# Where the sums of layer one's weight blocks are made: sixteen copies and sixteen adding transfers moved into layer zero's mixing

## The chip, the cores and the metric

One core of one Trainium2 chip. The metric is the device time of one execution in microseconds. TensorE is called PE here, VectorE DVE, ScalarE ACT, GpSimd POOL and SyncE SP, as in the profile.

## The reference

Two kinds of layers take turns, twice each: a linear attention (A) and a gated mixer (B). The change sits in B. "Layer zero" and "layer one" below are the first and the second pair.

```python
def _B_ref(x, w_in, w_sp, b_sp, w_out):          # x: 2048 x 512
    z = _gelu(jnp.einsum("bsd,df->bsf", x, w_in))
    z1 = z[..., :Fh]                              # 2048 x 896
    z2 = _layernorm(z[..., Fh:], axis=-1)         # 2048 x 896
    g = jnp.einsum("ts,bsf->btf", w_sp, z2) + b_sp[None, :, None]   # w_sp: 2048 x 2048
    return jnp.einsum("bsf,fd->bsd", z1 * g, w_out)

x = x + _A_ref(_layernorm(x, axis=-1), A_wqkv, A_wo)
x = x + _B_ref(_layernorm(x, axis=-1), B_w_in, B_w_sp, B_b_sp, B_w_out)
x = x + _A_ref(_layernorm(x, axis=-1), A_wqkv, A_wo)
x = x + _B_ref(_layernorm(x, axis=-1), B_w_in, B_w_sp, B_b_sp, B_w_out)
```

All is in float32. Each product runs as three passes on PE over values split in two: a high part that ACT copies into PE's format and a low part that DVE makes by subtraction (`split`, `mm3`, `acc`).

## The kernel before, in words

The order of the instructions on each engine is the order in which the program names them; nothing reorders them. An engine that waits holds up all that stands behind it on that engine, and so does SP, from whose queue nearly all transfers are issued. Tiles come from numbered slots that are given out in turn: 22 pages (`pg`, 256 KB), 6 quads (`qd`), 4 large ones (`bg`) and 8 banks of PSUM.

A pair of layers has four stages: `P1` (queries, keys and their sums), a transition, `P2` (the rest of attention, then z1 and z2), and `P4` (the mixing with `w_sp`, then the product with `w_out`). Before the first `P1` stands a start of its own.

The mixing is done with seven products in place of eight, called P1 to P7 in `P4.ORDER` (P2, P1, P6, P7, P4, P5, P3), over half matrices. Some of the products need sums of blocks of `w_sp`. These sums are made once: in layer zero, `Sums.tick` loads blocks, adds them on POOL and stores them (`s` tiles). In layer zero each product has 8 steps, 56 in all. In layer one the products P2 and P4 are divided once more (`DIVIDED`): each becomes seven smaller ones with 14 steps. These need sums of quarter blocks: for P2 and for P4 there are four sums (m = 1 to 4), each in two parts (q). `Sums.halve` makes them in DRAM, without an engine that computes: SP's queue copies a block of `w_sp` to a tile `hP2...` or `hP4...`, and POOL's queue then sends an adding transfer that adds another block, or another sum, to it (m = 2 takes the sum of m = 1, m = 4 that of m = 2). That makes 16 copies and 16 adds of 512 KB each. In the profile they appear as `hP<-in_wsp_dram` and `hP<-hP`.

Where `halve` is called before: eight copies (P2's) after output products 0 to 7 of layer zero and eight adds (P2's) after products 8 to 15, in `join`; P4's copies in steps 3 to 10 of layer one's `P1`; P4's adds in steps 4 to 11 of layer one's `P2`.

A step g of the mixing (`P4.run`) does this, in this order: `fetch(g + 4)` asks SP for the weight block four steps ahead; `sp(g + 2)` splits the block that is needed two steps ahead (`wsp`: ACT at L889, DVE at L890) and the rows of z2 for it (`zsp`); `mm(g)` runs 24 matmuls (18 in P6, P7 and P3) at L1055 to L1057; in steps 0 to 18 a `Sums.tick`; and `tick` multiplies one finished unit of g with z1 on POOL (`gate`, L1093) and asks for the next z1 page. A quad is free for the next load when `wsp` has split it. In the eight steps of P3 `wpiece` also loads one piece of `w_out` and splits it at once.

After the steps come 16 output products `o(i)` with `zsplit` two ahead of them (L109 on ACT, L112 on DVE), an addition to x at L1163 and a store at L1165. In layer zero `join(i, nxt)` follows each: it loads x tiles, query and key weights (`wk` at i = 8, `wq` at i = 10, four pieces each) and splits them for layer one's `P1`.

In layer one `P4.run` first asks for steps 0 to 2, then runs what is left of z1 (`p2.f()`, seven products at this point) beside the first splits of z, then asks for step 3, for the four bias rows (`loadb`, L1086, each one spread over 128 partitions) and for the steps from 4 on.

Of the kernel before, what the change touches and what calls it, by code (L numbers as in the profile page):

```python
# [12 lines left out]
AF = mybir.ActivationFunctionType  # L13
OP = mybir.AluOpType
# [38 lines left out]
DIVIDED = ((), ("P2", "P4"))  # L53
# [3 lines left out]
def mixer_kernel(ctx: ExitStack, tc: tile.TileContext, x_in, wqkv, wo_d, win1_d, win2_d, wsp_d, bsp_d, wout_d,  # L57
# [45 lines left out]
    def behind(ins, other):  # L103

        tc.add_manual_dep(ins.ins, other.ins.name, mybir.DependencyInfo(
            mybir.DependencyClass.Sync, mybir.DependencyReason.DATA))
# [149 lines left out]
    class P1:  # L256
# [180 lines left out]
        def run(self, sums):  # L437
            side = deque([self.win2] * NF)
            ND = NT - DEFER
            for s in range(1, NT + 2):  # L440
                self.loadx(s + 3)
                self.turn.load(s + 1)
                if 2 <= s < NT:
                    self.T_high(s)
                if s == 1:
                    if not self.kb:
                        self.K(0)
                    self.K(1)
                elif 2 < s <= NT:
                    self.K(s - 1)  # L450
                self.ln_a(s + 2)
                if 2 <= s < NT:
                    self.T_low(s)
                if s <= NT:
                    self.K_phi(s - 1)
                if s <= ND:
                    self.Q(s - 1)
                if s == NT + 1:
                    self.late()
                if s <= NT:  # L460
                    self.xsplit(s - 1)
                    self.K_split(s - 1)
                self.ln_b(s + 2)
                if s <= ND:
                    self.Q_phi(s - 1)
                if s >= 2:
                    self.Gmm(s - 2)
                if s == NT + 1:
                    self.late_phi()
                if s == 6:  # L470
                    self.wv, self.wo = (quads.get([P, 4, 512]) for _ in range(2))
                    nc.sync.dma_start(self.wv, wqkv[:, 1024:1536].rearrange("(c p) f -> p c f", p=P))
                    nc.sync.dma_start(self.wo, wo_d.rearrange("(c p) f -> p c f", p=P))
                if self.L == 1 and 3 <= s < 11:
                    sums.halve(13 + s)
                if s > 3 and side:
                    side.popleft().piece()
                if s > 2 and side:
                    side[0].fetch()
# [64 lines left out]
    class P2:  # L544
# [152 lines left out]
        def run(self, sums):  # L697
            w1 = self.win1
            for s in range(1, NT + 3):
                self.loadx(s + 1)  # L700
                self.qturn.load(s + 1)
                if s in self.qturn.by_pe:
                    self.c(s - 1)
                    self.b_high(s)
                    self.c2(s - 1)
                    self.p1.late_phi_b()
                    self.b_low(s)
                    if s >= 2:
                        self.d_high(s - 2)
                        self.d_low(s - 2)  # L710
                    self.p1.late()
                    self.c3(s - 1)
                    self.a2(s + 2)
                    self.p1.late_phi_a()
                    self.a(s + 3)
                else:
                    if s < NT:
                        self.b_high(s)
                    self.a2_den(s + 2)
                    if s < NT:  # L720
                        self.b_low(s)
                    if s <= NT:
                        self.c(s - 1)
                        self.c2(s - 1)
                    if s == NT:
                        quads.put(*self.W2)
                        pages.put(self.zbc)
                    self.a2_mul(s + 2)
                    late = s - 2 in self.xturn.by_pe
                    if late:  # L730
                        self.d_high(s - 2)
                        self.d_low(s - 2)
                    if s <= NT:
                        self.c3(s - 1)
                    self.a(s + 3)
                    if s <= NT + 1 and not late:
                        self.d_high(s - 2)
                        self.d_low(s - 2)
                if s >= 4:
                    self.e4(s - 4)  # L740
                self.xturn.load(s - 1)
                if s >= 3:
                    self.e(s - 3)
                    self.e2(s - 3)
                    self.e3(s - 3)
                self.f()
                self.f()
                self.fq.extend(self.fnext)
                self.fnext = []
                w1.piece(True)  # L750
                w1.fetch()
                if self.L == 0 and s > 4:
                    sums.tick()
                if self.L == 1 and 3 < s < 12:
                    sums.halve(20 + s)
                if s >= NT + 1:
                    self.p4.fetch(s - NT - 1)
            self.e4(NT - 1)
            self.win2.free()


    class Sums:
# [3 lines left out]
        def __init__(self):  # L766
            self.s = {(m, k): dram.tile([P, 2, 512], F32, name=f"s{m}_{k}") for m in range(1, 5) for k in range(HT)}
            self.todo = deque((k, j, h) for k in range(HT) for j in range(2) for h in range(2))
            self.ahead = deque(self.todo)
            self.raw, self.made, self.done = {}, [], []  # L770
            self.slots = pages
            self.parts, self.halves = [], {}
            for p in DIVIDED[1]:
                for q in range(2):
                    for m in range(1, 5):
                        self.halves[p, m, q] = dram.tile([2, P, 512], F32, name=f"h{p}_{m}_{q}")
            self.parts = [(what, p, m, q) for p in DIVIDED[1] for what in ("copy", "add") for m in (1, 3, 2, 4)
                          for q in range(2)]

        def fetch(self):  # L780
# [2 lines left out]
                at = ((j, k), (j, k + HT), (2 + j, k)) if h == 0 else ((2 + j, k + HT),)  # L783
                self.raw.setdefault((k, j), []).extend(load(wsp_d[n, s], self.slots) for n, s in at)

        def halve(self, n):

            if n >= len(self.parts):
                return
            what, p, m, q = self.parts[n]  # L790
            row = 2 if p == "P2" else 0
            j, s = {1: ((1, 0), (1, 4)), 3: ((0, 0), (1, 0)), 2: ((0, 0), None), 4: ((0, 4), None)}[m][what == "add"] or (0, 0)
            src = wsp_d[row + j, HT + s + 2 * q:HT + s + 2 * q + 2]
            if what == "copy":
                nc.sync.dma_start(self.halves[p, m, q], src)
            else:
                if m in (2, 4):
                    src = self.halves[p, m // 2, q]
                nc.gpsimd.dma_start(self.halves[p, m, q], src, accum_op=OP.add, max_dma_last_dim=4096)

        def store(self):

# [30 lines left out]
    class P4:  # L833
# [50 lines left out]
        def wsp(self, g):  # L884
            if g >= len(self.steps):
                return
            r = self.raw.pop(g)
            w = quads.get([P, 2, 2, 512], F32R)
            nc.scalar.activation(w[:, 0], r, AF.Copy)  # L889
            nc.vector.tensor_sub(w[:, 1], r, w[:, 0].bitcast(F32))  # L890
            quads.put(r)
            self.w[g] = w
# [277 lines left out]
        def run(self, nxt):  # L1170
            p2 = self.p2
            self.fetch(2)
            self.sp(0)
            ahead = deque()
            if self.div:
                self.zpart(0)
# [12 lines left out]
            p2.win1.free()  # L1189
            self.sp(1)  # L1190
            self.fetch(3)
            if self.div:
                self.loadb()
            self.gb = [bigs.get([P, NF, 512]) for _ in range(NCHK)]
            n = len(self.steps)
            for g in range(n):
# [11 lines left out]
                    self.sp(g + 2)  # L1208
                if g < 19:
                    self.sums.tick()  # L1210
                if g == 3 and not self.div:
                    self.loadb()
                if p in self.div:
# [29 lines left out]

        def join(self, i, nxt):

            self.sums.halve(i)
            if i in (5, 6, 7, 10):
                nxt.loadx((5, 6, 7, 10).index(i))
            if i in (7, 8, 9):
                nxt.ln_a(i - 7)  # L1250
                nxt.ln_b(i - 7)
            if i in (8, 10):
                for _ in range(4):
                    (nxt.wk if i == 8 else nxt.wq).fetch()
            if i in (11, 12):
                nxt.turn.load(i - 11)
            if 10 <= i < 14:
                nxt.wk.piece()
            if 11 <= i < 15:
                nxt.wq.piece()  # L1260
            if i == 14:
                nxt.T(0)
            if i == 15:
                nxt.T(1)
# [46 lines left out]
```

## Time and profile before

| | |
|---|---|
| runs shown | 1403.86, 1406.55 and 5764.37 us, median 1406.55 |
| the profiled execution | 1403.85 us, span 1402.1 us, mean granted clock 0.995 |
| PE busy | 1380.4 us, 98% of the span |
| DVE, ACT, POOL busy | 889.9, 587.1, 398.8 us |
| transfers | 248.76 MB, 177 GB/s over the span |
| of these, on POOL's queue | 8.39 MB, 3.5% of the time of 16 DMA engines |

The span runs from the first to the last instruction. Layer zero's mixing ends and its output products begin at about 624 us, layer one's `P1` begins at 716 us, layer one's mixing at 1056 us. A row of the timeline shows start, duration, engine, line, operation, written tile `<-` read tiles, shapes, count, and in brackets the idle time of the engine just before it with what ended it. SPq and POOLq rows are issues of transfers; a row `DMA` in the chain is a transfer on its way.

### The profile page before, as it was taken

How to read it: one execution, taken by the hardware profiler on the slowest of the kernel's cores; microseconds unless marked ns; L12 is line 12 of the kernel's file. 1: busy time of each engine (PE TensorE's matmuls, PEld its weight loads, DVE VectorE, ACT ScalarE, POOL GpSimd, SP SyncE). 2: the span in 40 equal slices, each digit the busy share in tenths (PEclk: the TensorE clock that was granted, in tenths of full speed). 3: DMA queues.
4: the chain of work that ended last, by engine and by line, in shares of the span. 5: the costliest groups of instructions: out<-in, count | busy, mean ns of one | idle time of the engine just before them, and what ended most of it. 6: DMA issues, size and time to landing. Idle time of an engine off the chain costs nothing.

```text
span 1402.1 us, 17453 instructions
## 1 busy us (share of the span) xinstructions
PE 1380.4 (98%) x6182; PEld 1150.6 (82%) x6182; DVE 889.9 (63%) x1331; ACT 587.1 (42%) x893; POOL 398.8 (28%) x506
## 2 busy tenths in 40 slices
PE   9999999999999999999799999999999999999998
PEld 7888888888888888888578888888887888878887
DVE  6665868752688766563266658776436757886532
ACT  6664533343323333340156645443345323633420
POOL 3233455444367102131213233543110020021300
PEclk9999999999999999999899999999999999999999
DMA  5641267866988433347947522787336444454432
GB/s 163 194 120 54 97 225 249 270 217 212 331 306 301 173 120 113 129 180 255 246 151 237 198 68 81 188 241 198 131 115 203 151 161 162 148 176 150 172 120 90
DMA packets 148344, 248.76 MB, mean 177 GB/s; under 512 B 12448, under 2 KB 51104, under 8 KB 148000
## 3 DMA queue, kind: packets, MB, share of 16 engines
q1 hardware_dynamic: 145952, 239.26, 51.3%
q0 software_dynamic: 2304, 8.39, 3.5%
q8 instruction: 48, 0.79, 0.2%
q14 instruction: 40, 0.33, 0.1%
HBM read 179.70 MB, written 84.67 MB: 189 GB/s over the span
## 4 chain that ended last, share of the span: by engine, by line
PE 88%; DVE 4%; DMA 3%; ACT 2%; issue 1%; POOL 1%; SPq 1%; ACTq 0%; DVEq 0%; POOLq 0%
PE bank L125 17%; PE bank L123 17%; PE bank L124 17%; PE bank L1056 12%; PE bank L1057 12%; PE bank L1055 12%; DMA pg<-in_wqkv_dram 2%; DVE qd L890 1%; DVE st L186 1%; PE bank L517 1%; DMA qd<-hP 1%; PE bank L528 0%; DMA pg<-in_x_dram 0%; SPq L100 0%; ACT qd L889 0%
## 5 line engine op out<-in xcount | busy, mean ns | idle before, releaser
L1056 PE MATMUL bank<-qd,pg 128*128 128x512 f32 x784 | 305.6, 390 | 1.5 <-DVE qd L890 1.5
L1055 PE MATMUL bank<-qd,pg 128*128 128x512 f32 x784 | 305.3, 389 | 0.7 <-ACT qd L889 0.7
L1057 PE MATMUL bank<-qd,pg 128*128 128x512 f32 x784 | 305.2, 389 | 0.0
L890 DVE TENSOR_TENSOR qd<-qd,qd 128x1024 fp32r<-128x1024 f32 x124 | 168.9, 1363 | 137.1 <-ACT qd L889 137.0
L889 ACT ACTIVATE qd<-qd 128x1024 fp32r<-128x1024 f32 x124 | 131.1, 1057 | 191.9 <-PE bank L1057 151.7
L1093 POOL TENSOR_TENSOR bg<-bg,pg 128x512 f32<-128x512 f32 x56 | 83.5, 1511 | 409.0 <-DVE bg L1103 147.8
L1056 PEld LDWEIGHTS bank<-qd,pg 128*128 128x128 f32 x784 | 147.2, 188 | 33.9 <-DVE qd L890 3.4
L1055 PEld LDWEIGHTS bank<-qd,pg 128*128 128x128 f32 x784 | 147.2, 188 | 32.0 <-ACT qd L889 1.1
L1057 PEld LDWEIGHTS bank<-qd,pg 128*128 128x128 f32 x784 | 147.2, 188 | 30.8 <-DVE pg L929 0.4
L125 PE MATMUL bank<-qd,pg 128*128 128x512 f32 x384 | 149.7, 390 | 0.0
L199 ACT ACTIVATE pg<-pg,nb,rs 128x512 f32<-128x512 f32 x63 | 51.0, 810 | 172.4 <-POOL nb L193 172.3
L190 POOL TENSOR_SCALAR rs<-mv 128x1 f32<-128x1 f32 x96 | 27.2, 284 | 331.2 <-DVE mv L188 330.5
L123 PE MATMUL bank<-qd,pg 128*128 128x512 f32 x288 | 112.5, 391 | 0.3 <-DVE pg L112 0.2
L124 PE MATMUL bank<-qd,pg 128*128 128x512 f32 x288 | 112.3, 390 | 0.2 <-DVE qd L112 0.2
L809 POOL TENSOR_TENSOR pg<-pg,pg 128x512 f32<-128x512 f32 x64 | 93.3, 1458 | 55.9 <-DMA pg<-in_wsp_dram 48.0
L125 PE MATMUL bank<-wo,qd 128*128 128x512 f32 x224 | 89.0, 397 | 9.6 <-DVE qd L112 9.6
L123 PE MATMUL bank<-bg,qd 128*128 128x448 f32 x256 | 94.2, 368 | 0.4 <-ACT qd L109 0.4
L124 PE MATMUL bank<-bg,qd 128*128 128x448 f32 x256 | 93.6, 366 | 0.0
L125 PE MATMUL bank<-bg,qd 128*128 128x448 f32 x256 | 93.6, 365 | 0.1
L123 PE MATMUL bank<-wo,qd 128*128 128x512 f32 x224 | 88.5, 395 | 2.7 <-ACT qd L109 2.7
L124 PE MATMUL bank<-wo,qd 128*128 128x512 f32 x224 | 88.1, 393 | 0.0
L125 PE MATMUL bank<-qd,bg 128*128 128x512 f32 x224 | 87.5, 390 | 0.0
(137 smaller groups left out, 2555.3 us busy)
## 6 DMA issues: line engine op xcount, KB each, us to landing
qd<-s SPq DMA_DIRECT2D x64, 512.0 KB, 3.3
qd<-in_wsp_dram SPq DMA_DIRECT2D x44, 512.0 KB, 4.0
pg<-in_wsp_dram SPq DMA_DIRECT2D x64, 256.0 KB, 4.9
s<-pg SPq DMA_DIRECT2D x64, 256.0 KB, 4.5
pg<-x SPq DMA_DIRECT2D x64, 256.0 KB, 3.9
z<-pg SPq DMA_DIRECT2D x56, 256.0 KB, 3.0
pg<-z SPq DMA_DIRECT2D x56, 256.0 KB, 3.7
x<-pg SPq DMA_DIRECT2D x48, 256.0 KB, 3.3
```

Source lines behind the costliest of these rows:

```text
L123: nc.tensor.matmul(out, ah, bh, start=start, stop=False)
L124: nc.tensor.matmul(out, ah, bl, start=False, stop=False)
L125: nc.tensor.matmul(out, al, bh, start=False, stop=stop)
L190: nc.gpsimd.tensor_scalar(rs, mv[:, 1:2], LN_EPS, None, op0=OP.add)
L199: nc.scalar.activation(y, x, AF.Identity, bias=nb, scale=rs)
L809: nc.gpsimd.tensor_tensor(t, a, b, op=OP.add)
L889: nc.scalar.activation(w[:, 0], r, AF.Copy)
L890: nc.vector.tensor_sub(w[:, 1], r, w[:, 0].bitcast(F32))
L1055: m(out, h[:, o], w[:, 0, j, :], start=start, stop=False, skip_group_check=True)
L1056: m(out, h[:, o], w[:, 1, j, :], start=False, stop=False, skip_group_check=True)
L1057: m(out, l[:, o], w[:, 0, j, :], start=False, stop=stop, skip_group_check=True)
L1093: nc.gpsimd.tensor_tensor(u, u, z1, op=OP.mult)
```

## The change

The list of the parts is put in another order, all 16 copies first (P2's, then P4's), then all 16 adds. The three places that called `halve` drop it. It is called instead in layer zero's mixing, once in each of the steps 19 to 50, behind the matmuls of the step and ahead of its `tick`: copies in steps 19 to 34, adds in 35 to 50. Each add gets a dependency on the instruction `mark`, the ACT half of the latest weight split, so that POOL issues it only when ACT has come to that step. In layer one the bias rows are asked for right behind the first split, ahead of the rest of z1. PE, DVE and ACT run the same instructions in the same order as before; the copies move on SP's queue, the adds on POOL's, and from the bias rows on some pages have other numbers.

```diff
@@ P1.run
-                if self.L == 1 and 3 <= s < 11:
-                    sums.halve(13 + s)
@@ P2.run
-                if self.L == 1 and 3 < s < 12:
-                    sums.halve(20 + s)
@@ Sums.__init__
-            self.parts = [(what, p, m, q) for p in DIVIDED[1] for what in ("copy", "add") for m in (1, 3, 2, 4)
+            self.parts = [(what, p, m, q) for what in ("copy", "add") for p in DIVIDED[1] for m in (1, 3, 2, 4)
                           for q in range(2)]
@@ Sums.halve
-        def halve(self, n):
+        def halve(self, n, after):
-            if n >= len(self.parts):
+            if not 0 <= n < len(self.parts):
                 return
...
-                nc.gpsimd.dma_start(self.halves[p, m, q], src, accum_op=OP.add, max_dma_last_dim=4096)
+                behind(nc.gpsimd.dma_start(self.halves[p, m, q], src, accum_op=OP.add, max_dma_last_dim=4096), after)
@@ P4.wsp
-            nc.scalar.activation(w[:, 0], r, AF.Copy)
+            self.mark = nc.scalar.activation(w[:, 0], r, AF.Copy)
@@ P4.run
             self.fetch(2)
             self.sp(0)
+            if self.div:
+                self.loadb()
...
             self.sp(1)
             self.fetch(3)
-            if self.div:
-                self.loadb()
...
                 if g < 19:
                     self.sums.tick()
+                if nxt is not None:
+                    self.sums.halve(g - 19, self.mark)
@@ P4.join
-            self.sums.halve(i)
```

## The prediction

> **What bounds the kernel now.** I read the busy times first, then the stretches of 35 us, then the waits and the chain where a stretch was short of full.
>
> ```profile
> PE 1380.4 (98%) x6182; PEld 1150.6 (82%) x6182; DVE 889.9 (63%) x1331; ACT 587.1 (42%) x893; POOL 398.8 (28%) x506
> ```
>
> TensorE is busy for all but 21.7 us of the span of 1402.1, and the change leaves its instructions and their order as they were. So there is little to win: those 21.7 us, and what the clock loses after a stop. I then looked where they lie (columns: stretch, length, busy us and count of PE, PEld, DVE, ACT, POOL, granted clock, DMA share, GB/s).
>
> ```profile
> 525.00:560.00 35.00, 35.00 (x156) 29.01 (x155) 21.81 (x30) 10.94 (x13) 7.64 (x5) 1.00 0.35 119
> ...
> 595.00:630.00 35.00, 35.00 (x156) 28.99 (x155) 23.28 (x29) 16.61 (x23) 12.16 (x8) 1.00 0.48 173
> 630.00:665.00 35.00, 35.00 (x156) 29.01 (x155) 12.85 (x17) 2.87 (x3) 3.03 (x4) 1.00 0.78 263
> 665.00:700.00 35.00, 26.20 (x108) 21.23 (x108) 9.89 (x14) 7.08 (x9) 9.62 (x16) 0.85 1.00 239
> 700.00:735.00 35.00, 31.59 (x131) 25.41 (x130) 20.97 (x34) 17.97 (x29) 4.01 (x9) 0.95 0.47 154
> ...
> 910.00:945.00 35.00, 35.00 (x164) 30.34 (x163) 24.58 (x43) 16.06 (x27) 15.69 (x26) 1.00 0.87 236
> ```
>
> 665 to 735 holds 12.2 us of the idle time, at a lower clock, with DMA at 1.00. That is the output product of layer zero, where the first adding transfers run. In layer one's first stages (910 to 945), where the second half of them runs, TensorE is full: taking them out there wins nothing. The chain and the DVE's timeline tell what happened at 665:
>
> ```profile
> 673.05 13.88 DMA pg<-in_wqkv_dram
> 686.99 15.14 DMA pg<-in_wqkv_dram
> 702.24 0.64 ACT qd L109
> ```
>
> ```profile
> 671.37 0.69 DVE L1163 TENSOR_TENSOR pg<-pg,bank 128x512 f32<-128x512 f32 x1 [2.04 <-PE bank L125]
> 676.13 0.69 DVE L1163 TENSOR_TENSOR pg<-pg,bank 128x512 f32<-128x512 f32 x1 [1.81 <-PE bank L125]
> 693.13 0.69 DVE L1163 TENSOR_TENSOR pg<-pg,bank 128x512 f32<-128x512 f32 x1 [11.15 <-DMA pg<-x]
> ...
> 716.21 0.69 DVE L1163 TENSOR_TENSOR pg<-pg,bank 128x512 f32<-128x512 f32 x1 [1.47 <-PE bank L125]
> ```
>
> Line 1163 ends each of the 16 output products, one every 4.76 us until 676.13 (the eleventh; five follow). Then the loads of layer one's query and key weights take 14 and 15 us and a load of x is late too; ACT and DVE wait for them in front of the split (L109, L112) that feeds the next product. The last product should end at 676.13 + 5 x 4.76 = 699.93 and ends at 716.21: **16.3 us late**. The adding transfers stand beside it:
>
> ```profile
> 675.63 1.79 POOL L799 DMA_DIRECT2D hP<-in_wsp_dram  x2
> 676.79 1.46 POOL L799 DMA_DIRECT2D hP<-hP  x1
> 679.24 0.81 POOL L799 DMA_DIRECT2D hP<-hP  x1 [0.98 <-DMA hP<-in_wsp_dram]
> ```
>
> ```profile
> DMA to landing us min/median/max: 5.8/8.2/14.1
> ...
> q0 software_dynamic: 2304, 8.39, 3.5%
> ```
>
> Nothing paces them there: four are issued from 675.63 to 680.05, on top of the weight loads. The 16 of them hold all 16 DMA engines for 3.5% of 1402.1 us, so about 3.1 us each (an estimate, and from a crowded stage, so rather high).
>
> **The change, part by part.** *Taken out of the output stage:* 8 copies and 8 adds. Worth 16.3 us if nothing else is late. What is late next is seen from the product's own split on ACT and DVE:
>
> ```profile
> 676.44 0.94 ACT L109 ACTIVATE qd<-bg 128x896 fp32r<-128x896 f32 x1
> ...
> 677.48 1.09 DVE L112 TENSOR_TENSOR qd<-bg,qd 128x896 fp32r<-128x896 f32 x1 [0.66 <-ACT qd L109]
> ```
>
> ACT wants the first weight piece behind this split, at 677.4. Four weight loads are under way from 673.05; a 256 KB load without an add beside it lands in 3.2 us (row below), so they are there by about 678. DVE's work per product is 0.69 + 1.09 and two weight pieces of some 0.7, 3.2 us of 4.76. Bounds: 16.3 us won, or 16.3 - 5 where half of the late waits stay; I take **-16.3**, since the products before 676 ran at full pace with the same loads of x and stores.
>
> *Put into layer zero's mixing:* the copies at steps 19 to 34 (about 451 to 520), the adds at steps 35 to 50 (520 to 604), one a step. (The split at 536.78 below is the one made in step 38; steps of products 4 and 5, up to step 47, take 5.44 us as these two rows show, those of 6, 7 and 3 have 18 matmuls in place of 24 and take 4.08.) A copy goes to SP's queue behind that step's loads and waits for no engine; an add goes to POOL's queue and waits for ACT's split of that step (L889). Behind the add wait POOL's gates (L1093), and behind a gate the page that it frees; such pages are written again three steps later at the earliest, 12 us, so a gate held for one or two us is covered. The cover of the loads that feed the splits:
>
> ```profile
> 531.34 1.06 ACT L889 ACTIVATE qd<-qd 128x1024 fp32r<-128x1024 f32 x1 [1.78 <-PE bank L1057]
> 536.78 1.06 ACT L889 ACTIVATE qd<-qd 128x1024 fp32r<-128x1024 f32 x1 [1.79 <-PE bank L1057]
> ...
> L889 ACT ACTIVATE qd<-qd x37: 1043/1061/1066, 442.8 to 611.1; 128x1024 fp32r<-128x1024 f32 x37
> ...
>   PE bank L1057: 39.6, 24
> ...
> qd<-s SPq DMA_DIRECT2D x64, 512.0 KB, 3.3
> ...
> L890 DVE TENSOR_TENSOR qd<-qd,qd 128x1024 fp32r<-128x1024 f32 x124 | 168.9, 1363 | 137.1 <-ACT qd L889 137.0
> ```
>
> From 440 to 660 these splits wait for TensorE (24 times) and never for a transfer. A load is issued when the split three steps before it has freed its buffer, so it has three steps less the 2.4 us of that split (1.06 on ACT, 1.36 on DVE): 14 us at 5.44 a step, 10 us at 4.08. It needs 3.3. DMA in these stretches stands at 0.35, 1.9 us of a step of 5.44; with an add that is 5.0 of 5.44, 91%. A copy costs between 1.4 us ((0.78 - 0.48) x 35 / 7.4 copies, from the stretches at 630 and 595) and 3.7 us (all of the 0.78): below 14 and 10 either way. These parts cost 0.
>
> The price of an add's company shows in layer one, in two stretches of the DMA issues, without (876 to 884) and with one (904 to 914):
>
> ```profile
> pg<-x SPq DMA_DIRECT2D x1, 256.0 KB, 3.2
> ...
> pg<-x SPq DMA_DIRECT2D x1, 256.0 KB, 7.1
> ```
>
> About 4 us more for a load. That matters in one place, the last product's steps 48 to 50, where a piece of the output weight is loaded and split in the same step (`wpiece`), with ACT standing still until it lands:
>
> ```profile
> 596.27 0.38 SPq L100 DMA_DIRECT2D pg<-in_wout_dram  x1
> ...
> 600.30 0.63 ACT L109 ACTIVATE wo<-pg 128x512 fp32r<-128x512 f32 x1 [3.62 <-DMA pg<-in_wout_dram]
> 600.84 1.05 ACT L889 ACTIVATE qd<-qd 128x1024 fp32r<-128x1024 f32 x1
> ...
> 608.72 0.63 ACT L109 ACTIVATE wo<-pg 128x512 fp32r<-128x512 f32 x1 [3.84 <-DMA pg<-in_wout_dram]
> 609.26 1.05 ACT L889 ACTIVATE qd<-qd 128x1024 fp32r<-128x1024 f32 x1
> ```
>
> The split at 600.84 is for step 52, which starts at about 607.5 (536.8 + 10 x 5.44 + 4 x 4.08): some 4 us to spare after the 2.4 us that the split needs. A late split also frees its buffer late, SP's queue stops on it, and the piece behind it on SP is asked for late. Followed from step to step, 3 us more per piece costs 0 to 0.4 us of TensorE, 4 us costs 1 to 2.5, 6 us costs 5 to 6.5, 8 us costs 9 to 10.5 (the first where only pieces up to 606 are slowed, the second up to 612). I take **+1.5**, nearest to the row of 4 us; the bounds are 0 and +10.
>
> The Trainium skill, "DMA: Bandwidth & Descriptors", section on the anatomy of a SWDGE transfer, fits 2.0 us plus bytes over 436 GB/s; for 512 KB that is an estimate of 3.2 us. By it an add would be gone before the next step's load, this term would be 0 and the time 1386.5. The trace disagrees (5.8 to 14.1 us to landing), so I keep the row.
>
> *The bias rows of layer one asked for sooner.* Now four loads stand on SP's queue between two loads of the sums; the rows are SP's timeline, the chain, ACT's timeline and TensorE's waits from 1050 to 1090, and ahead of them one wait from 660 to 720 that is used further down:
>
> ```profile
> PE bank L123 <- ACT qd L109: 2.7, 1, 2.7
> ...
> 1057.94 1.92 SPq L1086 DMA_DIRECT2D pg<-in_bsp_dram  x4
> ...
> 1059.95 7.12 DMA qd<-hP
> ...
> 1067.09 1.06 ACT L889 ACTIVATE qd<-qd 128x1024 fp32r<-128x1024 f32 x1 [2.40 <-DMA qd<-hP]
> ...
> PE bank L1056 <- DVE qd L890: 0.8, 1, 0.8
> PE bank L1055 <- ACT qd L889: 0.7, 1, 0.7
> ```
>
> Moved ahead of seven remaining products of the first gate half, they go out at about 1045; the load of the sums goes out 2 us earlier and alone. It then has the 2.4 us that ACT waited, and the two waits of TensorE go: **-1.5**. The four pages are held longer, but those taken are free by then. Bounds 0 and -1.6.
>
> **Sum**, against the profiled execution's own 1403.85 us (span 1402.1 and 1.8 around it): -16.3 - 1.5 + 1.5 gives 1387.5. The runs shown are 1403.86, 1406.55 and one far outlier, so their median of 1406.55 stands 2.7 above the lower of the two; I put 0.5 on top: **1388**.
>
> **The rivals.** *The output weight's pieces come late.* For it: they are the one load with no cover. Against: only three adds meet them. At 6 to 8 us more, 5 to 10 us lost, and 1.4 us for the clock (16.3 less the 12.2 of idle time is 4 us over three stops): 1392 to 1399.
>
> The Trainium skill, "TensorE: Matmul & The Clock Gate", part on the clock gate, lets the clock fall only after some 3.4 us of idle; stops of 1 to 2 us would then cost themselves alone, and the 1.4 would drop out: 1390 to 1398. The trace leaves it open: after the wait of 2.7 us, itself close behind a longer one, 700 to 735 shows 0.95.
>
> *The weight loads at 672 stay slow without the adds.* For it: x loads and stores and eight weight pieces remain. Against: 0.78 with copies did not slow TensorE. It would leave some 5 us: 1393.
>
> *The adds fill the DMA engines in the mixing (slower).* At 3.1 us an add the step is 91% full. If beside the split loads an add takes 6 us, a step needs 7.9 us in place of 5.44 and TensorE waits for split loads: 2.5 us in 13 steps, 3.9 in three, 44 us, less 18: 1430. It decides from 3.5 us per add on (where a step is full), and eats the whole gain at about 4.7. For it: 8.2 us to landing. Against: 910 to 945 runs with adds at 0.87 and TensorE full.
>
> *The change brings only the bias rows' gain or nothing there:* 1386 to 1389.5, inside the forecast.
>
> **How the numbers follow.** Forecast 1384.5 to 1391: 0.70. Pieces late: 0.15 (1392 to 1399). Weight loads stay slow: 0.10. Adds fill the engines: 0.05. The range 1384 to 1398 takes in the forecast and most of the two next. A difference of 2%, 28 us, is about what a measurement of this kernel can tell from no change. More than 28 us faster would need more than all the idle time and slow clock: 0.01. More than 28 us slower is a part of the last case: 0.03. Within: 0.96.
>
> **What would show it right or wrong.** Right: no adds after 620; the weight loads land in under 6 us; line 1163 keeps 4.76 us to its sixteenth; 630 to 735 full. The splits L889 from 440 to 610 still wait for TensorE. The load of the sums at the start of layer one's mixing lands in about 4 us. Wrong: waits of L889 or L890 for `qd` transfers in steps 35 to 50, ACT's waits for the output weight above 6 us and a PE wait at 607 to 620, or a hole at the layers' border that names the weights again.

## The result, and the profile after

The changed kernel takes 1387.49 us (median of 1386.75, 1388.24, 1392.31 and 1386.45) against 1405.2 us for the kernel before, run on the same chip. The ratio is 0.9884 [0.9852, 0.9917] (it leaves out the one far outlier of the kernel before, 5764 us, which that median still counts): 1.2% faster, so within 2%, and 0.5 us from the forecast of 1388. The profiled execution is the one of 1386.75 us. Its page, busy times and POOL's queue:

```profile
span 1384.9 us, 17460 instructions
...
PE 1376.4 (99%) x6182; PEld 1149.0 (83%) x6182; DVE 893.1 (64%) x1331; ACT 587.6 (42%) x893; POOL 396.7 (29%) x506
...
q0 software_dynamic: 2304, 8.39, 3.4%
```

TensorE's idle time fell from 21.7 to 8.5 us, with the same 6182 matmuls. The stretches of 35 us show where (columns as before: stretch, length, PE, PEld, DVE, ACT, POOL, granted clock, DMA share, GB/s):

```profile
595.00:630.00 35.00, 34.21 (x150) 27.80 (x149) 24.53 (x28) 16.33 (x24) 17.35 (x13) 1.00 0.71 214
630.00:665.00 35.00, 35.00 (x156) 28.99 (x155) 14.54 (x17) 3.59 (x4) 2.60 (x2) 1.00 0.42 140
665.00:700.00 35.00, 35.00 (x156) 29.01 (x155) 19.64 (x29) 12.62 (x18) 3.17 (x9) 1.00 0.66 214
700.00:735.00 35.00, 35.00 (x156) 28.97 (x156) 22.04 (x38) 22.74 (x38) 9.18 (x18) 1.00 0.44 128
```

The hole at 665 to 735 is gone: PE full, clock 1.00, DMA 0.66 and 0.44 in place of 1.00 and 0.47. What it cost stands one stage earlier: 595 to 630, full before, misses 0.79 us. DVE's timeline, the first and the last of the 16 output products (L1159 is the old L1163):

```profile
629.76 0.69 DVE L1159 TENSOR_TENSOR pg<-pg,bank 128x512 f32<-128x512 f32 x1 [2.64 <-PE bank L125]
...
701.16 0.69 DVE L1159 TENSOR_TENSOR pg<-pg,bank 128x512 f32<-128x512 f32 x1 [1.47 <-PE bank L125]
```

71.40 us apart, 15 x 4.76: the sixteenth product keeps the pace of the first. In the kernel before, the same two rows stood at 628.53 and 716.21, 87.68 us apart, so **16.28 us** are won here. Against that the first product comes 1.23 us later (629.76 against 628.53). The splits of steps 36 to 42 ran 0.10 us ahead of the kernel before, so the end of the mixing lost 1.33 us; further down, a loss in the mixing is always counted like this, against the splits ahead of it. The weight loads between 672 and 690, from the DMA issues (columns: transfer, queue, count, size, median us to landing; in the kernel before this row had 11.9, from 666 to 700):

```profile
pg<-in_wqkv_dram SPq DMA_DIRECT2D x8, 256.0 KB, 5.5
```

The moved adds, from the view of their line, L795 (what POOL waited for in front of them, us and times; and their landing):

```profile
  ACT qd L885: 116.2, 16
...
DMA to landing us min/median/max: 4.9/6.6/9.6
```

The splits from 440 to 660, from the view of L885 (what ACT waited for in front of them):

```profile
  PE bank L1053: 34.1, 24
```

POOL waited in front of each of the 16 adds for the split that it is tied to. The splits wait for TensorE, 24 times as before, and never for a transfer.

### The profile page after: what moved, and what is told of

Read it like the earlier page. It is cut to its first block, busy times and chain, and to the rows that moved or that the text cites. A ratio compares the mean times of both kernels' runs of the same rounds, so it can differ in the third digit from the quotient of the medians.

```text
span 1384.9 us, 17460 instructions
## 1 busy us (share of the span) xinstructions
PE 1376.4 (99%) x6182; PEld 1149.0 (83%) x6182; DVE 893.1 (64%) x1331; ACT 587.6 (42%) x893; POOL 396.7 (29%) x506
## 4 chain that ended last, share of the span: by engine, by line
PE 91%; DVE 4%; DMA 2%; ACT 2%; issue 1%; POOL 1%; SPq 0%; ACTq 0%; DVEq 0%; POOLq 0%
PE bank L125 18%; PE bank L124 18%; PE bank L123 18%; PE bank L1052 11%; PE bank L1053 11%; PE bank L1051 11%; DMA pg<-in_wout_dram 1%; DVE qd L886 1%; PE bank L515 1%; PE bank L526 0%; ACT qd L885 0%; DVE st L186 0%; PE bank L211 0%; DMA pg<-in_wqkv_dram 0%; DVE pg L112 0%
## 5 line engine op out<-in xcount | busy, mean ns | idle before, releaser
L885 ACT ACTIVATE qd<-qd 128x1024 fp32r<-128x1024 f32 x124 | 131.3, 1059 | 184.4 <-PE bank L1053 158.9
L125 PE MATMUL bank<-qd,bg 128*128 128x512 f32 x224 | 87.5, 391 | 0.0
L124 PE MATMUL bank<-qd,bg 128*128 128x512 f32 x224 | 87.4, 390 | 0.0
L123 PE MATMUL bank<-qd,bg 128*128 128x512 f32 x224 | 87.2, 389 | 0.0
L123 PE MATMUL bank<-wo,qd 128*128 128x512 f32 x224 | 87.1, 389 | 0.0
```

The source lines that it names most:

```text
L123: nc.tensor.matmul(out, ah, bh, start=start, stop=False)
L124: nc.tensor.matmul(out, ah, bl, start=False, stop=False)
L125: nc.tensor.matmul(out, al, bh, start=False, stop=stop)
L885: self.mark = nc.scalar.activation(w[:, 0], r, AF.Copy)
```

## The experiments

The theory: the hole at the layers' border comes from P2's eight adds alone, issued in a bunch on top of the weight loads; the copies cost nothing; in the mixing the adds cost only what they add to the output weight's pieces (steps 48 to 50); the bias rows are worth 1.5 us. The rivals: the copies, or the loads of x and of the weights themselves, make part of the hole; being in the output stage is what costs, not the bunching; the DMA engines in the mixing are close to full, so that more adds per step hold up the splits; the tie to a split does nothing.

### The hole: without the adds, without the copies, with paced adds, with the bias rows alone

These four are made from the kernel before, with its line numbers, and ran on one chip, beside a kernel before of 1404.42 us.

**P2's eight adds left out** (their sums then lack the added block).

```diff
-            self.sums.halve(i)
+            if i < 8:
+                self.sums.halve(i)
```

> The kernel before without the eight adding transfers of layer one's product P2 (they are left out, so these eight sums stay plain copies); the eight copies stay in the output stage. My theory, that the adds alone slow the weight loads there: the sixteen ends of the output product (L1163) keep 4.76 us, the two weight loads land in under 7 us, and the time falls by about 16 us, to 1387.5. Rival, that the copies or the eight weight pieces themselves are slow: at least 5 us of the hole stays, 1393 or more.

Measured: 1387.17 us, ratio 0.9877 [0.986, 0.9893]. Two stretches of this kernel:

```profile
665.00:700.00 35.00, 35.00 (x156) 29.00 (x155) 19.88 (x29) 12.60 (x18) 2.11 (x6) 1.00 0.64 210
700.00:735.00 35.00, 35.00 (x156) 29.01 (x155) 23.01 (x40) 24.40 (x40) 9.15 (x18) 1.00 0.49 158
```

DVE's timeline, its first and last output product:

```profile
627.80 0.69 DVE L1163 TENSOR_TENSOR pg<-pg,bank 128x512 f32<-128x512 f32 x1 [2.63 <-PE bank L125]
...
699.20 0.69 DVE L1163 TENSOR_TENSOR pg<-pg,bank 128x512 f32<-128x512 f32 x1 [1.48 <-PE bank L125]
```

71.40 us again, with the eight copies, the x loads and the weight loads all still there. The whole hole is the adds'. In these two stretches this kernel and the changed one are alike: TensorE full, DMA 0.64 and 0.49 against 0.66 and 0.44.

**P2's copies moved to mixing steps 19 to 26, the adds left.**

```diff
+                if nxt is not None and 19 <= g < 27:
+                    self.sums.halve(g - 19)
...
-            self.sums.halve(i)
+            if i >= 8:
+                self.sums.halve(i)
```

> The kernel before with the eight copies of layer one's P2 moved into layer zero's mixing (steps 19 to 26); the eight adds stay in the output stage. My theory, that the adds make the hole: the time stays at 1404 within 2 us. Rival, that copies and adds together fill the DMA engines, the copies ending only just ahead: the hole shrinks by a third or more, 1398 or less.

Measured: 1402.23 us, ratio 0.9985 [0.9975, 0.9994]. The hole is there whole; two stretches:

```profile
630.00:665.00 35.00, 35.00 (x156) 29.00 (x155) 13.43 (x16) 2.87 (x3) 3.60 (x6) 1.00 0.42 144
665.00:700.00 35.00, 25.91 (x107) 20.94 (x106) 9.89 (x14) 7.09 (x9) 9.01 (x15) 0.85 1.00 239
```

TensorE's waits from 640 to 740 (us in total, times, longest):

```profile
PE bank L125 <- DVE qd L112: 9.8, 2, 9.1
```

Without the copies DMA falls from 0.78 to 0.42 at 630 to 665 and nothing is won: TensorE was full in that stretch before, so a lower DMA share there was worth nothing.

**Each add in the output stage tied to that product's addition (L1163, here L1165).**

```diff
-                nc.gpsimd.dma_start(self.halves[p, m, q], src, accum_op=OP.add, max_dma_last_dim=4096)
+                d = nc.gpsimd.dma_start(self.halves[p, m, q], src, accum_op=OP.add, max_dma_last_dim=4096)
+                if after is not None:
+                    behind(d, after)
...
-            nc.vector.tensor_add(x, x, b)
+            self.mark = nc.vector.tensor_add(x, x, b)
...
-            self.sums.halve(i)
+            self.sums.halve(i, self.mark)
```

> The kernel before with each of the eight adds in the output stage tied to the end of its own output product (L1163), so that they go out one every 4.76 us from about 667 on and not four within 5 us. If bunching makes the hole (my theory, half of it): an add lands in about 8 us, the weight loads in about 8 us, TensorE loses 3 to 6 us there and the time is 1391 to 1395. Rival, that adds beside the weight loads cost the same however they are paced: 1402 to 1406. The other end, that pacing alone is enough: 1388 to 1390.

Measured: 1391.76 us, ratio 0.9908 [0.9893, 0.9923]. The output products take from 628.17 to 704.13, 75.96 us, so 4.56 us are lost in place of 16.3. The landing of the eight adds, from the view of their line, 640 to 720:

```profile
DMA to landing us min/median/max: 8.3/8.5/9.6
```

The stretch with the loss:

```profile
665.00:700.00 35.00, 32.68 (x137) 26.54 (x136) 16.29 (x23) 12.12 (x17) 7.75 (x13) 0.95 0.98 269
```

TensorE's only wait from 660 to 740:

```profile
PE bank L125 <- DVE qd L112: 2.3, 1, 2.3
```

TensorE's timeline around it:

```profile
685.09 0.39 PE L123 MATMUL bank<-wo,qd 128*128 128x512 f32 x1
685.32 0.39 PE L124 MATMUL bank<-wo,qd 128*128 128x512 f32 x1
688.03 0.53 PE L125 MATMUL bank<-wo,qd 128*128 128x512 f32 x1 [2.32 <-DVE qd L112]
...
690.48 0.63 PE L125 MATMUL bank<-wo,qd 128*128 128x512 f32 x1
690.91 0.63 PE L123 MATMUL bank<-wo,qd 128*128 128x512 f32 x1
```

And DVE's row just ahead of the stop:

```profile
686.28 0.69 DVE L1165 TENSOR_TENSOR pg<-pg,bank 128x512 f32<-128x512 f32 x1 [5.71 <-DMA pg<-x]
```

The same adds in the same stage, but one a product: 11.7 of the 16.3 us come back. So the bunch was most of the damage, and the company of single adds beside the loads of this stage the rest. The load that came too late was not one of the weights, which landed in 7.3 us, but a page of x (median 10.7 us, 666 to 700; 5.0 in the changed kernel): DVE stood 5.71 us for it, with the next product's split queued behind. Of the 4.56 us, 2.32 are the stop. Most of the rest is a slow clock behind it: the matmuls start up to 0.43 us apart (690.48 to 690.91) in place of 0.23 (685.09 to 685.32) until 691.8, which adds up to 1.7 us.

**The bias rows sooner, and nothing else.**

```diff
             self.sp(0)
+            if self.div:
+                self.loadb()
...
             self.fetch(3)
-            if self.div:
-                self.loadb()
```

> The kernel before with only the bias rows of layer one asked for sooner. My theory: the load of the sums at step 0 of layer one's mixing lands in about 4 us in place of 7.1, the two waits of TensorE (0.7 and 0.8 us) go, 1.5 us less in the profiled execution, 1402.3. Rival, that the waits only move to another load: the span within 0.5 us of 1402.1.

Measured: 1400.9 us, ratio 0.9973 [0.9962, 0.9984], 3.5 us less in the median. In its profiled execution the hole happened to be 14.6 us, so the time is no measure of the bias rows; their own stage is. From the last output product to the span's end it takes 683.8 us (1397.5 - 713.72), the kernel before 685.9 (1402.1 - 716.21), the kernel without P2's adds 686.0 (1385.2 - 699.20), the changed one 683.7 (1384.9 - 701.16). The last output product of the kernel with the bias rows sooner:

```profile
713.72 0.69 DVE L1163 TENSOR_TENSOR pg<-pg,bank 128x512 f32<-128x512 f32 x1 [1.48 <-PE bank L125]
```

The bias rows are worth **2.1 us**. With them moved, taking P4's copies and adds out of layer one's first stages is worth nothing (683.8 with them there, 683.7 without).

### The mixing: the adds in other steps, doubled, untied; the bias rows back

These four are made from the changed kernel, with its line numbers, beside a kernel before of 1403.18 us on another chip.

**Copies two a step in 19 to 26, adds one a step in 27 to 42,** so that none meets the output weight's pieces.

```diff
-                if nxt is not None:
-                    self.sums.halve(g - 19, self.mark)
+                if nxt is not None and 19 <= g < 27:
+                    self.sums.halve(2 * (g - 19), self.mark)
+                    self.sums.halve(2 * (g - 19) + 1, self.mark)
+                if nxt is not None and 27 <= g < 43:
+                    self.sums.halve(g - 11, self.mark)
```

> The changed kernel with two copies a step in steps 19 to 26 and one add a step in steps 27 to 42, so that no add meets the pieces of the output weight in steps 48 to 55. My theory, that the adds of steps 47 to 50 cost about 1.2 us there: the first output product ends 1.2 us sooner (628.5 and not 629.76), the wait of ACT for the pieces falls from 4.6 to under 4 us, 1385.5. Adds in the steps of 18 matmuls are covered all the same (no wait of a split L885 for a transfer). Rival, that an add a step of 4.08 us fills the DMA engines: waits of L885 for transfers and 2 us or more lost between steps 27 and 35.

Measured: 1387.03 us, ratio 0.9886 [0.9871, 0.9901]. The loss beside the pieces is gone, but one of 0.67 us appears at steps 32 to 35. There two splits wait for a transfer (waits of L885, 440 to 660):

```profile
  DMA qd<-in_wsp_dram: 1.9, 2
```

Both splits (496.31 and 500.32) are made in the last of the short steps of 4.08 us, beside the adds. The time is the changed kernel's: 1.2 us less had been expected, and both the theory and the rival were right in part.

**Two adds a step in 35 to 42.**

```diff
-                if nxt is not None:
+                if nxt is not None and g < 35:
                     self.sums.halve(g - 19, self.mark)
+                if nxt is not None and 35 <= g < 43:
+                    self.sums.halve(16 + 2 * (g - 35), self.mark)
+                    self.sums.halve(17 + 2 * (g - 35), self.mark)
```

> The changed kernel with two adds a step in steps 35 to 42 in place of one in steps 35 to 50. By my price of 3.1 us an add these eight steps need 8.1 us of the DMA engines in 5.44 us: 21 us of work left over at their end; the cover of 14 us before a split is used up after some five steps, the splits wait for transfers, and TensorE loses 5 to 10 us: 1391 to 1396. If an add costs the engines 2 us or less, or the split loads pass the adds because each engine takes turns between the queues: no wait of a split, 1385 to 1387, the 1.2 us at the output weight won as well.

Measured: 1384.9 us, ratio 0.9874 [0.9857, 0.989]. The loss that was expected did not come; it was the lowest median of the four. Three stretches of 15 us:

```profile
525.00:540.00 15.00, 15.00 (x68) 12.43 (x67) 7.63 (x12) 4.96 (x6) 3.29 (x4) 1.00 1.05 254
540.00:555.00 15.00, 15.00 (x67) 12.39 (x67) 11.13 (x16) 4.33 (x5) 6.27 (x7) 1.00 1.03 237
555.00:570.00 15.00, 15.00 (x68) 12.42 (x67) 8.54 (x13) 5.08 (x6) 3.38 (x4) 1.00 1.06 260
```

The landing of the adds, from the view of L795:

```profile
DMA to landing us min/median/max: 6.0/9.8/17.1
```

The splits from 440 to 660, from the view of L885, the only engine or transfer that they waited for:

```profile
  PE bank L1053: 39.9, 25
```

The DMA engines are full here for 45 us and TensorE loses nothing. Most of the delay goes to the adds: the first kind (from `in_wsp_dram`) lands in 11.9 us in place of 7.1, a split load in 8.3 in place of 6.2 (medians of 525 to 580, against the changed kernel). A split load has 14 us, and nobody waits for an add but the next one. The adds are done before the output weight's pieces come. The rival was right here: for these eight steps, "It decides from 3.5 us per add on" in the prediction was wrong. More than eight such steps in a row were not tried.

**The adds untied.**

```diff
-                behind(nc.gpsimd.dma_start(self.halves[p, m, q], src, accum_op=OP.add, max_dma_last_dim=4096), after)
+                nc.gpsimd.dma_start(self.halves[p, m, q], src, accum_op=OP.add, max_dma_last_dim=4096)
```

> The changed kernel without the tie of each add to ACT's split. POOL then runs ahead: six adds go out as fast as the copies of P2 land (about 460 to 490), the rest in a bunch from about 550. My theory, that in the mixing the loads have 10 to 14 us of cover and the tie is therefore worth little: the same time within 2 us, 1385 to 1389, an add taking 10 us or more to land. Rival, that the tie is what keeps the adds harmless: splits wait for transfers and TensorE loses 5 us or more, 1392 or more.

Measured: 1389.41 us (1387.14 to 1390.7), ratio 0.9902 [0.9887, 0.9917], between what the theory and its rival had expected. The profiled execution is the slowest of the four, 1390.7 us; it loses 5.65 us in the mixing, at steps 28 to 35. The landing of the adds:

```profile
DMA to landing us min/median/max: 5.0/8.9/17.7
```

Two stretches of 15 us:

```profile
480.00:495.00 15.00, 13.06 (x55) 9.83 (x54) 5.06 (x7) 3.40 (x5) 0.81 (x1) 1.00 1.07 331
495.00:510.00 15.00, 13.11 (x56) 9.98 (x54) 10.09 (x15) 7.17 (x9) 0.00 (x0) 1.00 0.95 326
```

Three splits in ACT's timeline:

```profile
484.51 1.06 ACT L885 ACTIVATE qd<-qd 128x1024 fp32r<-128x1024 f32 x1 [4.28 <-DMA qd<-s]
...
490.19 1.06 ACT L885 ACTIVATE qd<-qd 128x1024 fp32r<-128x1024 f32 x1 [2.34 <-DMA qd<-s]
...
495.20 1.06 ACT L885 ACTIVATE qd<-qd 128x1024 fp32r<-128x1024 f32 x1 [1.62 <-DMA qd<-s]
```

And TensorE's waits from 440 to 520:

```profile
PE bank L1051 <- ACT pg L923: 2.4, 3, 1.2
PE bank L1051 <- DVE bg L1115: 1.7, 1, 1.7
```

Without the tie POOL runs ahead and issues adds from 463.9, among the copies. The split loads then land in 13.5 us (median, 462 to 486) with 10 us of cover, and the splits wait for them. This is the rival "the adds fill the engines", in one place: where copies, adds and loads meet in the short steps. The tie keeps the adds out of that place. In a usual execution it is worth less than these 5.65 us: the ratios of the medians are 0.9902 and, for the changed kernel, 0.9884.

**The bias rows back to their old place.** The edit is that of the bias rows alone, reversed.

> The changed kernel with the bias rows of layer one asked for where they were before. My theory: the two waits of TensorE at the start of layer one's mixing come back, the span is 1.5 to 2 us longer than the 1384.9 of the changed kernel. Rival: no difference, under 0.5 us.

Measured: 1389.2 us, ratio 0.9903 [0.9889, 0.9918]. From the last output product (701.7) to the end (1386.7) it takes 685.0 us, so the rows' place is worth 1.2 us here and not 2.1. The 0.9 us between the two was not separated: with the rows in their old place, this kernel, which has no copies and adds in layer one, is that much faster behind the last output product than the kernel before, and why was not tried. Its code up to the last output product is the changed kernel's, so it is a second profile of the mixing: it loses 2.34 us there, with ACT standing 6.7 us for the second piece of the output weight.

### The output weight's pieces: the term that varies

These three ran on a third chip, in 5 rounds, beside a kernel before of 1404.28 us.

**The changed kernel once more**, without an edit, to stand beside the next two.

> The changed kernel itself once more, beside the two others of this set, so that they can be compared on one chip: 1387.5 within 1 us, and again 1.3 us lost between steps 50 and 55.

Measured: 1388.1 us (1392.1, 1387.19, 1388.25, 1387.96), ratio 0.9884 [0.9865, 0.9904]. The profiled execution is the slowest, 1392.1 us. ACT's timeline, the first three pieces, in the changed kernel's first profile:

```profile
596.07 0.63 ACT L109 ACTIVATE wo<-pg 128x512 fp32r<-128x512 f32 x1 [3.52 <-DMA pg<-in_wout_dram]
...
600.97 0.64 ACT L109 ACTIVATE wo<-pg 128x512 fp32r<-128x512 f32 x1 [2.90 <-DMA pg<-in_wout_dram]
...
607.55 0.63 ACT L109 ACTIVATE wo<-pg 128x512 fp32r<-128x512 f32 x1 [4.57 <-DMA pg<-in_wout_dram]
```

The same three in this execution:

```profile
595.42 0.63 ACT L109 ACTIVATE wo<-pg 128x512 fp32r<-128x512 f32 x1 [3.57 <-DMA pg<-in_wout_dram]
...
600.30 0.63 ACT L109 ACTIVATE wo<-pg 128x512 fp32r<-128x512 f32 x1 [2.88 <-DMA pg<-in_wout_dram]
...
610.97 0.63 ACT L109 ACTIVATE wo<-pg 128x512 fp32r<-128x512 f32 x1 [8.68 <-DMA pg<-in_wout_dram]
```

Its waits of TensorE from 590 to 640:

```profile
PE bank L1051 <- ACT pg L923: 2.3, 1, 2.3
PE bank L1053 <- DVE pg L925: 1.1, 1, 1.1
```

And its stretch:

```profile
595.00:630.00 35.00, 31.28 (x124) 24.86 (x123) 21.71 (x24) 15.43 (x22) 14.20 (x11) 0.90 0.69 209
```

The third piece, asked for at 599.18, is used at 610.97, 11.8 us later; in the first profile it was asked for at 599.83 and used at 607.55, 7.7 us later. With this piece 4 us later, 7.36 us of the mixing are lost against 1.33. The adds beside it were slower too (9.0 us to landing against 7.3, medians from 590 to 606), and what made this execution's transfers slow was not found. Two of the eight executions of the changed kernel lie at 1392; the other one (1392.31) has no profile, so that it has the same cause is argued, not shown.

**Each piece asked for one step earlier.**

```diff
+        def wfetch(self, f):
+            if f < NF:
+                self.wraw = load(wout_d[f * P:(f + 1) * P, :])
+
         def wpiece(self, f):
-            r = load(wout_d[f * P:(f + 1) * P, :])
+            r = self.wraw
+            self.wfetch(f + 1)
...
                 self.tick()
+                if p == "P5" and k == HT - 1:
+                    self.wfetch(0)
```

> The changed kernel with each piece of the output weight asked for one step before the step that splits it, in both layers; the adds stay at steps 35 to 50. My theory, that the 1.3 us lost in steps 50 to 55 come from pieces that are split as soon as they are asked for while adds slow them: with a step of cover ACT no longer stands still for them (waits under 1 us), the first output product ends about 1.3 us sooner against the start of the mixing, 1385 to 1386.5. Rival, that the adds slow POOL's gates or the split loads there: ACT's waits go, the 1.3 us stays.

Measured: 1384.93 us (1384.27 to 1385.13), ratio 0.9863 [0.9847, 0.9879]. ACT's timeline, the same three pieces:

```profile
592.15 0.61 ACT L109 ACTIVATE wo<-pg 128x512 fp32r<-128x512 f32 x1
...
596.19 0.61 ACT L109 ACTIVATE wo<-pg 128x512 fp32r<-128x512 f32 x1
...
603.79 0.63 ACT L109 ACTIVATE wo<-pg 128x512 fp32r<-128x512 f32 x1 [3.43 <-DMA pg<-in_wout_dram]
```

And the stretch:

```profile
595.00:630.00 35.00, 35.00 (x156) 28.99 (x156) 28.83 (x29) 16.53 (x23) 17.16 (x13) 1.00 0.68 209
```

It had been expected that ACT's waits go, and they do not all go: the third, fourth and fifth piece still cost ACT 3.43, 3.54 and 1.54 us. But the first two cost nothing, ACT splits the first three pieces 3.8 to 4.8 us sooner than in the changed kernel's first profile, and TensorE never has to wait for a late one. The loss in the mixing is 0, and the spread falls from 5 us to 1.

**Two adds a step again.** The kernel of above, without an edit.

> Once more the changed kernel with two adds a step in steps 35 to 42, beside the changed kernel. If it is the better version by what its trace shows in the mixing (nothing lost): 1.3 us under the changed kernel on the same chip. If its lower time was chance at the kernel's start: the same within 0.5 us.

Measured: 1385.0 us (1384.57 to 1385.69), ratio 0.9865 [0.9848, 0.9881]. It ends the adds before the pieces begin and wins the same 3 us by the other way. Both versions beat the changed kernel on this chip, by 3.2 and 3.1 us in the median, more than the 1.3 us that had been expected. The one profile of the changed kernel on this chip, less its 7.36 us, comes to 1384.7 us, the time of these two; so its usual executions here seem to lose some 3 us in the mixing, but they have no profile.

## Why the prediction was right

**The output stage, -16.3: right.** 16.28 us measured, and the kernel without the adds shows that they alone made it. What the prediction named as late next was in time: the output products keep 4.76 us to the sixteenth, and the weight loads land in 5.5 us, in its "under 6". They do not land in 3.2 us, though, the row of a single load by which it reckoned them there by 678: ACT stands 4.91 us for one of them, up to 685.36, and TensorE stays full all the same.

**Copies and adds beside the split loads, 0: right, by the cover.** The splits from 440 to 610 wait for TensorE and never for a transfer. With an add a step DMA stands at 0.80, 0.88, 0.95 and 0.89 in the four stretches of 15 us from 525 on, where the prediction put 91%. The cover of 14 and 10 us was the right number to compare with: 8.3 us in the kernel with two adds a step stayed under 14 and cost nothing; 13.5 us in the untied kernel went over 10 and cost 5.65.

**The output weight's pieces, +1.5: the mechanism was right; that the number fits, 1.33, is luck.** Company was priced at 4 us. Here a piece took 7.8 us to land against 4.5 before (medians of the DMA issues from 590 to 606), so 3.3. But the term is not a constant: the kernel with the bias rows back loses 2.34 us in this place and the repeat 7.36. Both show the sign that the prediction gave for being wrong here: a wait of ACT for the output weight above 6 us (6.70 and 8.68) and a wait of TensorE between 607 and 620. The rival with a chance of 0.15, 1392 to 1399, is thus not another outcome of the kernel but a tail of its executions, seen in one profile. The bounds of 0 and +10 held both.

**The bias rows, -1.5: right mechanism, too small.** They are worth 2.1 us in layer one's part, beyond the bound of 1.6. The load of the sums did come early and alone, and from 1020 to 1090 TensorE has no wait left, as forecast. SP's timeline of the changed kernel:

```profile
1029.78 1.99 SPq L1082 DMA_DIRECT2D pg<-in_bsp_dram  x4
...
1042.46 4.43 SPq L867 DMA_DIRECT2D qd<-hP  x3
```

And ACT's, where the split waited 2.40 us before:

```profile
1046.58 1.06 ACT L885 ACTIVATE qd<-qd 128x1024 fp32r<-128x1024 f32 x1 [0.80 <-DMA qd<-hP]
```

The term was bounded by the two waits that TensorE's view names, 0.8 and 0.7 us. The stage lost 0.5 us more than these; no row names it. Bounding a stall by the named waits of one engine was the weak step; the length of the stage would have been the safer bound.

**The sum.** -16.3 + 1.3 - 2.1 from 1403.85 gives 1386.75, the profiled time; the half us put on for the median of the runs was about right (1387.49). That the forecast of 1388 is off by only 0.5 us is in part luck: the bias rows brought 0.6 us more than forecast, and the loss at the pieces varies by more than that from one execution to the next.

**The rivals.** "The weight loads stay slow without the adds" is out (5.5 us, no hole). "The adds fill the DMA engines" had its threshold wrong: full engines (1.05 for 45 us) delay the adds, which nobody waits for, and only a load whose landing exceeds its cover costs anything. Its sum was off as well: 13 steps over 5.44 us and three over 4.08 lose the 18 us from 4.4 us an add on, not 4.7. Of the Trainium skill's fit ("DMA: Bandwidth & Descriptors", anatomy of a SWDGE transfer), an estimate of 3.2 us for an add: no add here landed under 4.9 us, the median is 6.6, and the pieces paid for the adds' company, which the prediction put at nothing by that estimate; the row was the better price.

## What to carry to other kernels

The cover of a load is the time from its issue until its data are needed. A transfer that nobody waits for still costs what it does to the transfers beside it. So look for the loads there that have no cover, and place it where each has more cover than its landing time with company. Compare landing time with cover, not the DMA share with 1: TensorE stayed full beside engines at 1.05. Where a queue would run ahead and bunch such transfers, a tie to the engine that paces the stage spreads them, and a load used in the step in which it is issued is best asked for one step earlier.

## What the runs showed of the hardware

**A stop of 2.3 us was followed by a slow clock for 3.7 us.** In the paced kernel TensorE stops once, for 2.32 us, and its matmuls then start up to 0.43 us apart, not 0.23, from 688.03 to 691.8; the stop with what followed cost 4.56 us, about double. In the repeat of the changed kernel stops of 2.3 and 1.1 us, close together, brought the stretch's clock to 0.90. In the untied kernel, stops of at most 1.7 us left it at 1.00. In the kernel before, the matmuls were 0.23 us apart again from 698.4 to 700.7, ahead of the stop of 2.7 us and one of 0.75 behind it, and start 0.43 us apart from 705.8 to 708.4. These are few stops, and where between 1.7 and 2.3 us the limit lies, or whether it is a fixed one, they do not show. The Trainium skill, "TensorE: Matmul & The Clock Gate", part on the clock gate, lets the clock fall after an idle window of about 3.4 us; the measured stop of 2.32 us is shorter, so this rule does not hold here; for the stops of at most 1.7 us it does. The 1.4 us that the prediction kept for the clock is near the 1.7 lost behind this stop.

**An add from DRAM to DRAM holds the engines briefly and lands late.** 512 KB took 3.4% of 1384.9 us over 16 adds, 2.9 us of all 16 engines each, but landed in 4.9 to 9.6 us when paced one a step and in up to 17.7 us in a bunch. Beside them a 256 KB piece took 3.3 us longer (7.8 against 4.5, medians). The Trainium skill, "DMA: Bandwidth & Descriptors", section on SWDGE, HWDGE and iDMA, says that an engine takes its queues of the two kinds in turn; the kernel with two adds a step fits this, since both kinds grew there (split loads from 6.2 to 8.3 us, adds from 7.1 to 11.9) and neither starved; the turns themselves no trace here shows.
